# A rational activation rewritten in a scaled h: one square per unit, two output products, sums by accumulating transfers

## The chip, the cores and the metric

The kernel runs on one core of one Trainium2 chip. The metric is the device time of one execution in microseconds (us); lower is better. Three executions of the kernel before took 253.45, 253.46 and 253.82 us, median 253.46 us.

The core's engines work side by side, each through its own queue in order: TensorE (PE in the profile, its weight loads PEld), VectorE (DVE), ScalarE (ACT), GpSimd (POOL) and SyncE (SP). They wait for each other through semaphores. Transfers (DMA) are issued from the SyncE, ScalarE and GpSimd queues; those that add to what stands at their destination are issued from GpSimd here.

## The reference

Attention without softmax over a product of two sketches, and on its output a feed-forward layer whose activation is a rational function:

```python
def phi(x):                                   # x: (4, 4, 1088, 32), S1, S2: (8, 32)
    a = np.einsum('rd,bhsd->bhsr', S1, x)
    b = np.einsum('rd,bhsd->bhsr', S2, x)
    return np.einsum('bhsi,bhsj->bhsij', a, b).reshape(*x.shape[:-1], r * r)
q_p, k_p = (phi(q), phi(k))
kv = np.einsum('bhsf,bhsd->bhfd', k_p, v)
z = np.sum(k_p, axis=2)
num = np.einsum('bhsf,bhfd->bhsd', q_p, kv)
den = np.einsum('bhsf,bhf->bhs', q_p, z)[..., None] + 1e-06
attn_out = num / den

x = attn_out.transpose(0, 2, 1, 3).reshape(4352, 128)
h = x @ w_in                                  # w_in: (128, 2048)
P = a[0] + a[1] * h + a[2] * h * h + a[3] * h * h * h
Q = 1.0 + np.abs(b[0]) * np.abs(h) + np.abs(b[1]) * h * h
out = (P / (Q + 1e-6)) @ w_out                # w_out: (2048, 128)
```

## The kernel before

**Two halves that overlap.** The attention runs over four batches. For each, the keys (steps `K`) are turned, sketched, multiplied and summed into kv and z, and the queries (steps `Q`, in three or four pieces of tokens) are turned, sketched, multiplied with kv and z, divided and turned back into xT, which holds x with its 128 columns on the partitions (a ring of 1,536 tokens). The sketches of most query pieces go through DRAM: `dw` writes them, `dr` reads them back repeated over partitions. The feed-forward layer runs over 21 units. A unit is a stretch of tokens by a stretch of the 2,048 hidden columns; units 3 to 17 are 4,096 elements wide on each partition (512 tokens x 8 blocks of 128 columns, or 256 x 16), units 0 and 1 and 19 and 20 are 1,024 wide, units 2 and 18 are 2,048 wide.

**What a unit does.** The letters are those of the order below.
- `H`: TensorE makes h in parts of 1,024 elements into PSUM, in f32 (L518). `E`: ScalarE (or VectorE) copies a part to `hh` in bf16 (L272, L274).
- `U`: |h| on VectorE, by clearing the sign bit (L531). `W`: `w` = |b1| |h| + |b0| (L537, L539). `Y`: `w` times |h| (L554), so that w = |b1| h^2 + |b0| |h|. In units 6, 8, 10, 12 and 14 ScalarE instead takes a square of a scaled h (`D`, L544), and a transfer adds |h| to it (`M`, L550).
- `L`, `X`: r = 1 / (1 + w) on ScalarE, as Exp(-Ln(1 + 1e-6 + w)) (L576, L581). All Ln share one buffer.
- `P`: `g` = a3 h + a2 (L559, L562). `V`: `g` times h (L572). `A`, in units 7 to 15: a transfer adds a1, a constant tile in DRAM called `ones`, to it (L568). `S`: s = h r (L585). `G`: `g` times s (L589).
- `Or`, `Os`, `Og`: TensorE adds r, s and g times scaled copies of w_out to the output of the tokens in PSUM, 128 x 128 x 128 each (L620, L632). Units 7 to 15 have a1 in g and need only r and g, so two output products; most others need three. Units 16 and 17 need four, on r, s, s h and s h^2 (`B`, `C`, L594, L601), with two more scaled copies of w_out.
- `ST`, `OUT`: the output leaves PSUM and is stored.

**What sets the order.** All work is written out in one list of steps, `ORDER` (L40 to L78): a step's letter, the batch, piece or unit, the part, and the engine (`.a` ScalarE, `.d` VectorE) where there is a choice. Nothing else schedules. Each engine takes its own steps in this order, so a step that waits holds up all that follow on the same engine. The bf16 tiles stand in pools of their own: three buffers of `hh`, two of `w`, four of `g`, two of `r`, two of `s`, one of `u`, 14 of 8 KB per partition in all. `early` (L165) issues the first loads, `absolute`, `nearest` and `square_root` (L712 to L733) make the constants from a and b, `w_part` (L687) scales the copies of w_out.

Of the kernel before, what the change touches and what calls it, by code (L numbers as in the profile page):

```python
# [40 lines left out]
I0 I11 I2 I3 I7 Z10 Z3 K0.T0 K0.T1 SS0 K0.s0 K0.T2 F1.k K0.s1 K0.c1.a Q0.1.T Q0.1.sk Q0.1.c.a K0.c0.d I9 Q0.0.T  # L41
Q0.0.sk Q0.0.c.a K0.f0 K0.p0 K0.f1 Q0.2.T Q0.3.T Q0.0.f Q0.1.f K0.p1 I4 Q0.2.sk K1.T2 K0.k0.a Q0.0.p I8 KA0 K1.T1
K1.s1 Q0.0.pl.d Q0.0.r Q0.0.x Q0.2.c.a K1.c1.a Q0.0.b Q0.1.p K1.T0 Q0.1.pl.d I5 Q0.1.r Q0.0.kk.a I6 Q0.2.dw Q0.3.sk
F1.q Q0.3.c.d H0.0 Q0.1.x F1.v KA1 KA2 Q0.1.b AB0 K1.s0 w0.a Q0.2.dr w2.d w4.d E0.0.a H1.0 RT0 I10 U0.0.d K1.f1 W0.0.a
Y0.0 K1.c0.a K1.f0 H2.0 F2.k E1.0.a U1.0.d L0.0 Q0.1.kk.a Q1.2.T Q1.1.T H2.1 P0.0.d X0.0 W1.0.d E2.0.a Or0.0 E2.1.a
Q1.1.sk P1.0.a K1.p0 Q1.0.T Q1.0.sk Q1.0.c.a Y1.0 L1.0 Q0.3.dw V0.0 Q1.0.dw K1.p1 K1.k0.a S0.0 U2.0.d Q0.2.f Os0.0
Q0.2.p G0.0 X1.0 Q1.2.sk Or1.0 Q0.2.pl.d F2.q Q0.2.r Q0.2.x Q0.2.b Q0.3.dr V1.0 W2.0.a Q0.2.kk.d P2.0.d w3.a S1.0 V2.0
Og0.0 K2.T2 w5.a H3.0 w1.a E3.0.a H3.1 Q1.1.c.a Q1.2.c.a K2.T0 Q1.0.dr G1.0 Y2.0 E3.1.a L2.0 K2.s0 K2.c0.d K2.T1 H3.2
P3.0.d E3.2.a H3.3 E3.3.a Og1.0 X2.0 Q2.0.T Q2.0.sk H4.1 E4.1.a Q1.1.dw Q2.1.T P3.1.a Q2.2.T K2.f0 Q1.2.dw H4.0 E4.0.a
H4.2 E4.2.a U3.0.d W3.0.d Q2.0.c.a Y3.0 Os1.0 Q0.3.f Q1.0.f Q0.3.p K2.s1 V3.0 Q1.0.p Q1.0.pl.d Q0.3.pl.a Q0.3.r Q1.0.r  # L50
# [31 lines left out]
def kernel(  # L82
# [702 lines left out]
```

## Time and profile before

| what | us |
|---|---|
| median of the runs | 253.46 |
| runs, lowest and highest | 253.45, 253.82 |
| profiled execution: span from the first to the last instruction | 251.9 |
| busy: h_ps products (L518) | 127.5 |
| busy: ScalarE copies of h (L272) | 69.2 |
| busy: ScalarE Exp (L581) | 64.4 |
| busy: ScalarE Ln (L576, two groups) | 65.2 |
| busy: VectorE products s (L585) | 39.4 |
| GpSimd's accumulating transfers | 28, 512 KB each |

For the profiled execution the page gives its span, and no time around it. A row of a group gives line, engine, operation, output and inputs, sizes, a count, then busy time and the mean length of one, then the idle time just ahead of them and what ended it. A length is from start to end of one instruction; neighbours on one engine overlap a little, so that starts stand closer together than the lengths say. A row in order of time gives start and length in us. "DMA to landing" is the time from a transfer's issue to its last byte's arrival.

### The profile page before, as it was taken

How to read it: one execution, taken by the hardware profiler on the slowest of the kernel's cores; microseconds unless marked ns; L12 is line 12 of the kernel's file. 1: busy time of each engine (PE TensorE's matmuls, PEld its weight loads, DVE VectorE, ACT ScalarE, POOL GpSimd, SP SyncE). 2: the span in 40 equal slices, each digit the busy share in tenths (PEclk: the TensorE clock that was granted, in tenths of full speed). 3: DMA queues.
4: the chain of work that ended last, by engine and by line, in shares of the span. 5: the costliest groups of instructions: out<-in, count | busy, mean ns of one | idle time of the engine just before them, and what ended most of it. 6: DMA issues, size and time to landing. Idle time of an engine off the chain costs nothing.

```text
span 251.9 us, 6008 instructions
## 1 busy us (share of the span) xinstructions
PE 242.7 (96%) x2565; PEld 170.2 (68%) x2565; DVE 239.7 (95%) x231; ACT 231.5 (92%) x177; POOL 31.9 (13%) x61
## 2 busy tenths in 40 slices
PE   8999999999999999999999999999999889999994
PEld 2778844655575776756666578554675579999983
DVE  2889999999999999999999999999999999999993
ACT  2249999998999999999999999999999999999991
POOL 2140000000003000220242020350115300000000
PEclk9999999999999999999999999999999999999999
DMA  6986673378637468688759817899182995000300
GB/s 193 278 272 170 214 228 133 74 188 204 191 90 197 86 203 219 127 154 144 129 136 185 170 21 152 165 199 200 23 170 41 202 209 134 3 0 3 83 21 26
DMA packets 21834, 35.48 MB, mean 141 GB/s; under 512 B 2992, under 2 KB 13872, under 8 KB 21808
## 3 DMA queue, kind: packets, MB, share of 16 engines
q0 software_dynamic: 4032, 14.68, 31.3%
q1 hardware_dynamic: 16768, 19.80, 28.0%
q10 hardware_dynamic: 1008, 0.62, 1.1%
q8 instruction: 20, 0.33, 0.5%
q14 instruction: 6, 0.05, 0.1%
HBM read 26.12 MB, written 3.74 MB: 119 GB/s over the span
## 4 chain that ended last, share of the span: by engine, by line
ACT 36%; DVE 25%; PE 22%; issue 13%; DMA 2%; ACTq 0%; DVEq 0%
ACT hh L272 10%; PE h_ps L518 10%; ACT r L581 9%; ACT ln L576 8%; DVE g L572 4%; DVE w L554 4%; DVE g L589 3%; PE out_ps L632 3%; DVE u L531 3%; ACT w L544 3%; PE att_ps L433 2%; DVE s L585 2%; PE att_ps L337 2%; DMA s_raw<-in_S_dram 2%; DVE w L539 2%
## 5 line engine op out<-in xcount | busy, mean ns | idle before, releaser
L518 PE MATMUL h_ps<-xT,w_in_sb 128*128 128x512 f32 (+1 forms) x320 | 127.5, 539 | 2.4 <-ACT hh L272 1.8
L518 PEld LDWEIGHTS h_ps<-xT,w_in_sb 128*128 128x128 f32 x320 | 57.2, 190 | 45.6 <-issue 36.1
L272 ACT CAST hh<-h_ps 128x1024 bf16<-128x1024 f32 x66 | 69.2, 1122 | 1.0 <-PE h_ps L518 0.9
L581 ACT ACTIVATE r<-ln 128x4096 bf16<-128x4096 f32 (+2 forms) x21 | 64.4, 3068 | 0.1
L576 ACT ACTIVATE ln<-w 128x4096 f32<-128x4096 bf16 (+2 forms) x16 | 45.7, 2854 | 0.4 <-DVE w L554 0.4
L585 DVE TENSOR_TENSOR s<-hh,r 128x4096 bf16<-128x4096 bf16 (+2 forms) x21 | 39.4, 1874 | 0.1
L572 DVE TENSOR_TENSOR g<-g,hh 128x4096 bf16<-128x4096 bf16 (+2 forms) x19 | 34.7, 1830 | 0.0
L589 DVE TENSOR_TENSOR g<-g,s 128x4096 bf16<-128x4096 bf16 (+2 forms) x19 | 34.5, 1831 | 0.1
L632 PEld LDWEIGHTS <-r 128*128 128x128 bf16 x512 | 29.9, 98 | 6.8 <-issue 5.7
L632 PEld LDWEIGHTS <-g 128*128 128x128 bf16 x512 | 29.7, 98 | 4.5 <-issue 3.8
L554 DVE TENSOR_TENSOR w<-w,u 128x4096 bf16<-128x4096 bf16 (+2 forms) x16 | 27.9, 1746 | 0.0
L632 PE MATMUL out_ps<-w_out,r 128*128 128x128 bf16 x416 | 25.7, 219 | 0.0
L632 PE MATMUL out_ps<-w_out,g 128*128 128x128 bf16 x416 | 25.4, 219 | 0.0
L550 POOL DMA_DIRECT2D w<-u x10 | 9.9, 1195 | 110.5 <-DVE q_sb L366 58.8
L568 POOL DMA_DIRECT2D g<-ones x18 | 16.5, 1156 | 45.8 <-PE out_ps L632 19.3
L531 DVE TENSOR_SCALAR u<-hh 128x4096 uint16<-128x4096 uint16 (+2 forms) x21 | 21.2, 1010 | 1.0 <-ACT hh L272 1.0
L576 ACT ACTIVATE ln<-w,scale 128x4096 f32<-128x4096 bf16 x5 | 19.5, 3907 | 0.0
L544 ACT ACTIVATE w<-hh,root 128x4096 bf16<-128x4096 bf16 x5 | 19.2, 3848 | 0.0
L632 PEld LDWEIGHTS <-s 128*128 128x128 bf16 x288 | 16.7, 98 | 3.1 <-issue 2.9
L559 DVE TENSOR_SCALAR g<-hh,a_k 128x4096 bf16<-128x4096 bf16 (+2 forms) x16 | 18.6, 1166 | 0.0
L539 DVE TENSOR_SCALAR w<-u,b_abs 128x4096 bf16<-128x4096 bf16 (+2 forms) x13 | 15.3, 1174 | 0.1
L433 PE MATMUL att_ps<-kvz,a_all 128*64 128x66 f32 x288 | 10.9, 224 | 0.6 <-DVE a_all L417 0.2
(97 smaller groups left out, 219.0 us busy)
## 6 DMA issues: line engine op xcount, KB each, us to landing
g<-ones POOLq DMA_DIRECT2D x18, 512.0 KB, 8.1
w<-u POOLq DMA_DIRECT2D x10, 512.0 KB, 6.5
k_sb<-in_k_dram SPq DMA_DIRECT2D x4, 544.0 KB
a_all<-sk_d SPq DMA_DIRECT2D x6, 352.0 KB
b_all<-sk_d SPq DMA_DIRECT2D x12, 176.0 KB
q_sb<-in_q_dram SPq DMA_DIRECT2D x3, 544.0 KB
v_sb<-in_v_dram SPq DMA_DIRECT2D x10, 144.0 KB
out_dram<-out_sb SPq DMA_DIRECT2D x19, 64.0 KB
```

The costliest lines, as they stand in the source:

```text
L272: nc.scalar.copy(out=out, in_=in_)
L518: nc.tensor.matmul(t[:, (x - part * m) * tl:(x - part * m + 1) * tl], lhsT=w_in_sb[:, (f0 + x) * 128:(f0 + x + 1) * 128], rhs=xT[:, p:p + ...
L531: nc.vector.tensor_scalar(out=at(i, "u", *c).bitcast(U16), in0=at(i, "hh", *c).bitcast(U16), scalar1=0x7FFF, scalar2=None, op0=AX.bitwise_and)
L539: nc.vector.tensor_scalar(out=at(i, "w", *c), in0=at(i, "u", *c), scalar1=ab1, scalar2=ab0, op0=AX.mult, op1=AX.add)
L544: nc.scalar.activation(out=at(i, "w", *c), in_=at(i, "hh", *c), func=ACT.Square, scale=root)
L554: nc.vector.tensor_mul(out=at(i, "w", *c), in0=at(i, "w", *c), in1=at(i, "u", *c))
L572: nc.vector.tensor_mul(out=at(i, "g", *c), in0=at(i, "g", *c), in1=at(i, "hh", *c))
L576: nc.scalar.activation(out=ln_sb[:, :ce - c], in_=at(i, "w", c, ce), func=ACT.Ln, bias=1.0 + 1e-6, scale=scale0 if i in SQ else 1.0)
L581: nc.scalar.activation(out=at(i, "r", c, ce), in_=ln_sb[:, :ce - c], func=ACT.Exp, scale=-1.0)
L585: nc.vector.tensor_mul(out=at(i, "s", *c), in0=at(i, "hh", *c), in1=at(i, "r", *c))
L589: nc.vector.tensor_mul(out=at(i, "g", *c), in0=at(i, "g", *c), in1=at(i, "s", *c))
L632: nc.tensor.matmul(outs[t0][:, m * 128:(m + 1) * 128], lhsT=z[:, m * 128:(m + 1) * 128], rhs=w, start=first and j == 0 and m == 0, stop=le ...
```

## The change

**The algebra.** The denominator of each attention output is multiplied by b0/b1 (absolute values, kept off zero), so that x, and with it h, comes out multiplied by b1/b0. With this scaled h, |b0| |h| + |b1| h^2 of the reference is (b0^2/b1) (|h| + h^2), and the numerator is a0 + outer h (constant + h + cubic h^2). So one square serves both:
- `N`: w = h^2, on VectorE (16 units) or ScalarE (units 1, 4, 5, 7, 11).
- `U`: u = |h|, as before. `M` (15 units) or `Y` (6): u plus w, by transfer or on VectorE.
- `L`, `X`: as before, Ln with the scale b0^2/b1 in all units.
- `P`: g = cubic w + constant, on VectorE in all units. `A` (15 units) or `V` (6): g plus h, by transfer or on VectorE; `ones` is gone, the transfer's source is the unit's own `hh`.
- `S`: h times r, now written over `hh`. `G`: g times that.
- `Or`, `Og` alone in every unit: r with a0 w_out, g with outer w_out. `Os`, `Om`, `On`, `B`, `C`, `D`, `W` and the third to fifth copy of w_out are gone.

**Buffers.** The pools of `hh`, `u`, `w`, `g`, `r`, `s` become one pool of 14 tiles of the same size; `w`, `u`, `g` and `r` are taken from it by step as `hh` is.

**Start.** b_sb is loaded ahead of everything else on the SyncE queue (`I12`), and its absolute value (`C0`) is taken on ScalarE before the load of S2 is issued there. The other constants (`C1` to `C6`) are some 18 small operations on GpSimd and two on VectorE, spread over the first steps.

**Order.** The whole of `ORDER` is new: which copies of h VectorE makes (8 parts in place of 2), where the attention's steps stand, and where the units'.

```diff
-HH, WB, GB, RB, SB, LN, AB, RING = 3, 2, 4, 2, 2, 1, 3, 1536
+BUFS, LN, AB, RING = 14, 1, 3, 1536
-TWO = (7, 8, 9, 10, 11, 12, 13, 14, 15)
-SQ = (6, 8, 10, 12, 14)
-FOUR = (16, 17)
+SMALL, TINY = 1e-10, 1e-12
 ORDER = """
-I0 I11 I2 I3 I7 Z10 Z3 K0.T0 K0.T1 SS0 K0.s0 K0.T2 F1.k K0.s1 K0.c1.a Q0.1.T Q0.1.sk Q0.1.c.a K0.c0.d I9 Q0.0.T
...
+I12 C0 I11 I0 I2 I3 I7 I8 I9 C1 K0.T0 Q0.1.T K0.T2 SS0 K0.T1 C2 Q0.0.T C3 C4 Z10 K0.s0 K0.s1 Q0.1.sk Q0.0.sk
+K0.c0.a K0.c1.a K0.f0 K0.f1 Q0.2.T Q0.3.T Q0.0.c.a K0.p0 Q0.2.sk Q0.3.sk K0.p1 Q0.1.c.a Q0.2.c.a w2.a K0.k0.a C5
+Q0.0.f Q0.3.c.a Q0.0.p Z3 I4 F1.k F1.q Q0.0.pl.a Q0.0.r Q0.0.x Q1.0.T Q1.1.T Q0.0.b Q1.0.sk Q1.1.sk Q0.2.dw I6
+Q0.3.dw I5 Q0.2.dr Q1.0.c.d K1.T1 Q0.1.f K1.T0 K1.T2 Q1.1.c.d Q1.2.T Q0.2.f Q0.0.kk.a H0.0 H2.1 Q0.1.p Q0.2.p
...
+Or6 X7 E10.2.a Q2.1.kk.a E10.0.a S7 Q3.1.f Q3.0.pl.d L8 H11.0 H11.1 Og6 A8 M9 E11.0.a E11.1.a ST6.a X8 N10.d U10
+P10.d Q3.0.r G7 S8 Q3.0.x G8 H11.2 Or7 H11.3 Or8 Q3.1.p Og7 Og8 Q2.2.b A10 M10 E11.2.a E11.3.a L9 N11.a ST8.a
...
+N15.d U15 S13 Og11 H16.3 H16.2 G13 E16.3.a E16.2.a H16.1 H16.0 Og12 M14 A14 M15 L14 E16.1.a E16.0.a ST12.a X14
+U16 N16.d H17.0 H17.2 E17.2.a E17.0.a P15.d S14 P16.d V15 G14 M16 Or13 H17.3 H17.1 L15 E17.1.a E17.3.a A16 H18.0
+H18.1 Og13 Or14 Og14 X15 E18.1.a E18.0.a L16 X16 N17.d U17 S15 N18.d P17.d U18 G15 P18.d S16 G16 M17 OUT12 OUT10
+Or15 H19.0 Or16 H20.0 Og15 Og16 E19.0.a L17 M18 A17 E20.0.d U19 N19.d N20.d P19.d U20 P20.d V19 Y20 M19 X17 L18
+X18 ST16.a L19 ST14.a X19 S17 G17 A18 L20 X20 S18 A20 S19 G18 G19 S20 G20 Or17 Or18 Og17 Or19 Og18 Or20 Og19
+Og20 OUT16 OUT14 ST17.a ST20 OUT17 OUT20
 """
...
             if eng == "d":
-                nc.vector.tensor_scalar(out=self.den[:tl, :T * H], in0=self.nv[:, :, D], scalar1=1e-6, scalar2=None,
-                                        op0=AX.add)
+                nc.vector.tensor_scalar(out=self.den[:tl, :T * H], in0=self.nv[:, :, D], scalar1=1e-6, scalar2=back_by[:tl],
+                                        op0=AX.add, op1=AX.mult)
...
     def at(i, key, c, ce):
-        w = UW if key in WHOLE else 2048
-        k = c // w
-        if (key, k) not in live[i]:
-            pool, bufs = homes[key]
-            live[i][key, k] = pool.tile([128, w], BF, name=key, bufs=bufs)
-        assert ce <= (k + 1) * w
-        return live[i][key, k][:, c - k * w:ce - k * w]
+        if key not in live[i]:
+            live[i][key] = late.tile([128, UW], BF, name="x", bufs=BUFS)
+        return live[i][key][:, c:ce]
...
+    def square(i, eng):
+        c = whole(i)
+        if eng == "a":
+            nc.scalar.activation(out=at(i, "w", *c), in_=at(i, "hh", *c), func=ACT.Square)
+        else:
+            nc.vector.tensor_mul(out=at(i, "w", *c), in0=at(i, "hh", *c), in1=at(i, "hh", *c))
...
+    def by_transfer(i, to, of):
+        for x in range(0, width(i), 2048):
+            e = min(x + 2048, width(i))
+            nc.gpsimd.dma_start(out=at(i, to, x, e), in_=at(i, of, x, e), accum_op=AX.add)
+
+    def by_vector(i, to, of):
+        c = whole(i)
+        nc.vector.tensor_add(out=at(i, to, *c), in0=at(i, to, *c), in1=at(i, of, *c))
+
+    def factor(i, eng):
+        c = whole(i)
         if eng == "d":
-            nc.vector.tensor_scalar(out=at(i, "g", *c), in0=at(i, "hh", *c), scalar1=a3, scalar2=a2,
+            nc.vector.tensor_scalar(out=at(i, "g", *c), in0=at(i, "w", *c), scalar1=cubic, scalar2=constant,
                                     op0=AX.mult, op1=AX.add)
...
+    def logarithm(i):
+        c, ce = whole(i)
+        nc.scalar.activation(out=ln_sb[:, :ce], in_=at(i, "u", c, ce), func=ACT.Ln, bias=1.0 + 1e-6, scale=slope)
+
+    def scaled(i):
+        c = whole(i)
+        nc.vector.tensor_mul(out=at(i, "hh", *c), in0=at(i, "hh", *c), in1=at(i, "r", *c))
...
+    stages = {"H": hidden, "E": evac, "N": square, "U": absolute, "M": lambda i: by_transfer(i, "u", "w"),
+              "Y": lambda i: by_vector(i, "u", "w"), "P": factor, "A": lambda i: by_transfer(i, "g", "hh"),
+              "V": lambda i: by_vector(i, "g", "hh"), "L": logarithm, "X": inverse, "S": scaled, "G": rational,
+              "Or": lambda i: gather(i, 0), "Og": lambda i: gather(i, 1), "ST": turn_out, "OUT": store, "F": fetch,
+              "I": early, "w": w_part, "Z": turn, "C": coefficients, "SS": sketch_weights}
```

More of the change, by code (lines that the diff above doesn't have):

```diff
@@ L46 @@
[L46 to L50, printed above, removed]
@@ L636, in turn_out @@
+        left[t0] -= n
+        for m, x in ([(m, x) for m in range(2) for x in range(n)] if end else
+                     [(m, x) for x in range(n) for m in range(tl // 128)]):
+            c = x * tl + m * 128
+            nc.tensor.matmul(outs[t0][m], lhsT=at(i, ("r", "g")[y], c, c + 128), rhs=w_sb[y][:, f0 + x, :],
+                             start=first and x == 0 and (end or m == 0),
+                             stop=left[t0] == 0 and x == n - 1 and (end or m == tl // 128 - 1))
     def turn_out(i, eng="d"):
@@ L717, in nearest @@
         if n == 0:
[L718 to L721 removed]
+            nc.scalar.activation(out=b_sb, in_=b_sb, func=ACT.Abs)
         elif n == 1:
[L723 to L727 removed]
```

291 lines of the change are left out of this document (94 added, 197 removed).

## The prediction

> **What bounds the kernel now.** I read the page's busy shares first, then busy time by stretches, then the groups by line with shapes kept apart, then the order in time of TensorE, ScalarE and SyncE at the places that the change touches.
>
> ```profile
> span 251.9 us, 6008 instructions
> PE 242.7 (96%) x2565; PEld 170.2 (68%) x2565; DVE 239.7 (95%) x231; ACT 231.5 (92%) x177; POOL 31.9 (13%) x61
> q0 software_dynamic: 4032, 14.68, 31.3%
> q1 hardware_dynamic: 16768, 19.80, 28.0%
> 0.00:20.00 20.00, 17.94 (x232) 12.08 (x233) 12.90 (x32) 6.76 (x16) 5.54 (x33) 1.00 0.82 245
> 60.00:100.00 40.00, 40.00 (x408) 25.67 (x406) 39.96 (x39) 39.57 (x30) 1.98 (x2) 1.00 0.64 165
> 100.00:140.00 40.00, 39.93 (x403) 27.10 (x401) 40.00 (x28) 40.00 (x26) 9.69 (x10) 1.00 0.78 147
> 240.00:252.00 12.00, 7.73 (x131) 7.12 (x128) 7.82 (x12) 5.96 (x8) 0.00 (x0) 1.00 0.09 23
> ```
>
> In the stretches the columns are PE, PEld, DVE, ACT, POOL, clock, DMA share, GB/s. Between 20 and 240 us TensorE, VectorE and ScalarE are all filled, so no engine alone is the bound: whatever takes work from one of them is lost unless the other two shrink as well. The clock is full throughout and is no part of the argument. The runs' median, 253.46 us, stands 1.6 us above this span (253.46 - 251.9), and I add that at the end.
>
> **Engine sums of the change.** TensorE loses every product with s (288 + 32 loads of s), nothing else.
>
> ```profile
> L632 PEld LDWEIGHTS <-s 128*128 128x128 bf16 x288 | 16.7, 98 | 3.1 <-issue 2.9
> L620 PE MATMUL end_ps<-w_out,s 128*128 128x128 bf16 x32 | 2.1, 219 | 0.0
> 216.76 1.95 PE L632 MATMUL end_ps<-w_out,r 128*128 128x128 bf16 x32
> 218.55 1.95 PE L518 MATMUL h_ps<-xT,w_in_sb 128*128 128x256 f32 x8
> 220.33 1.95 PE L632 MATMUL out_ps<-w_out,g 128*128 128x128 bf16 x32
> ```
>
> The starts are 1.79 us apart both for 32 output products (56 ns each) and for one 1024-wide part of the hidden product. So 320 x 0.056 = 17.9 us go.
>
> VectorE, by rows:
>
> ```profile
> L585 DVE TENSOR_TENSOR s<-hh,r 128x4096 bf16<-128x4096 bf16 x15 | 34.2, 2279 | 0.1
> L559 DVE TENSOR_SCALAR g<-hh,a_k 128x4096 bf16<-128x4096 bf16 x12 | 15.9, 1334 | 0.0
> L274 DVE CAST hh<-h_ps 128x1024 bf16<-128x1024 f32 x2 | 2.4, 1217 | 0.0
> L539 DVE TENSOR_SCALAR w<-u,b_abs 128x4096 bf16<-128x4096 bf16 (+2 forms) x13 | 15.3, 1174 | 0.1
> L554 DVE TENSOR_TENSOR w<-w,u 128x4096 bf16<-128x4096 bf16 (+2 forms) x16 | 27.9, 1746 | 0.0
> L572 DVE TENSOR_TENSOR g<-g,hh 128x4096 bf16<-128x4096 bf16 (+2 forms) x19 | 34.7, 1830 | 0.0
> L589 DVE TENSOR_TENSOR g<-g,s 128x4096 bf16<-128x4096 bf16 (+2 forms) x19 | 34.5, 1831 | 0.1
> ```
>
> Gone are W (15.3), the third and fourth products of units 16 and 17 (four of 2.28 us, 9.1), the copies of weights (2.2) and Y and V as they were (27.9 + 34.7). New are squares of eleven full, two half and three quarter units (29.6), seven full and five quarter sums that stay on VectorE (19.4), five more P (5.1), two more G (4.8), six more evacuations (7.3) and small copies (2): 68.2 against 88.9, about -21. The square and the sum are not in the trace; both read and write tiles of the shape of L585, and I take its 2279 ns. Below, a read of one tile twice could cost as little as the 1334 ns of L559 (11 x 0.95 = -10 us); above, nothing in these rows is dearer.
>
> ScalarE loses six evacuations, the W and P that it did, one full square less a quarter, a weight copy and copies of xT, some 24 us by the lengths of single instructions, some 22 without their overlap. It gains the scale in every Ln:
>
> ```profile
> L544 ACT ACTIVATE w<-hh,root 128x4096 bf16<-128x4096 bf16 x5 | 19.2, 3848 | 0.0
> L562 ACT ACTIVATE g<-hh,a_k 128x1024 bf16<-128x1024 bf16 (+1 forms) x4 | 6.7, 1683 | 0.0
> L576 ACT ACTIVATE ln<-w 128x4096 f32<-128x4096 bf16 x10 | 37.5, 3748 | 0.0
> L576 ACT ACTIVATE ln<-w,scale 128x4096 f32<-128x4096 bf16 x5 | 19.5, 3907 | 0.0
> ```
>
> Ten full Ln x 0.16 = 1.6 us, so about -20. All three sums fall by 18 to 21 us. If the whole of it came through, the time would be 253.5 - 18 to 20 = 234 to 235.
>
> **What does not come through.** The new order has to be walked. TensorE's work other than the parts of h and the output products is 242.7 - 68 x 1.785 - 1408 x 0.0558 = 42.7 us (68 parts; 544 products with r, 544 with g, 320 with s), and all of it stands before unit 16 in the new order. Before the end of step H16.2 the order has 58 parts (103.5 us) and 672 output products (37.5), and the first 20 us hold 2.1 us of idling (20 - 17.94). Sum: 42.7 + 103.5 + 37.5 + 2.1 = 185.8. The same sum for the kernel before (58 parts, 864 products) gives 196.6 for the start of H16.2; the trace has 197.2, so I add 0.6.
>
> ```profile
> 197.17 3.70 PE L518 MATMUL h_ps<-xT,w_in_sb 128*128 128x512 f32 x8
> ```
>
> From there ScalarE has, in the new order, ten evacuations, four full Ln and Exp, one half-width pair, two quarter pairs and three copies out of PSUM.
>
> ```profile
> 218.07 3.62 ACT L581 ACTIVATE r<-ln 128x4096 bf16<-128x4096 f32 x1
> 221.59 1.91 ACT L272 CAST hh<-h_ps 128x1024 bf16<-128x1024 f32 x2
> 223.39 3.63 ACT L576 ACTIVATE ln<-w 128x4096 f32<-128x4096 bf16 x1
> 231.47 1.92 ACT L576 ACTIVATE ln<-w 128x2048 f32<-128x2048 bf16 x1
> 245.06 1.06 ACT L581 ACTIVATE r<-ln 128x1024 bf16<-128x1024 f32 x1
> 248.58 0.64 ACTq L661 DMA_DIRECT2D out_dram<-last  x1
> ```
>
> From start to start that is 0.9 an evacuation, 3.6 a full Ln, 3.52 a full Exp, 1.8 and 1.0 for the narrower ones, 0.5 a copy: 9.1 + 28.5 + 3.7 + 3.9 + 1.6 = 46.8. ScalarE reaches E16.2 earlier by its own sum than TensorE does (its rows before that step, with 13 us of idling at the start, come to some 176), so some 10 us of its saving turn into waits for h; and after H16.2 TensorE has 10 parts and 416 products, 41 us, less than ScalarE's 46.8, and its last products wait for ScalarE's results, so that its own saving ends there. The path is TensorE up to unit 16, then ScalarE. Exp of unit 17 also takes the buffer that product Og16 reads; G16, Og15 and Og16 end about 1.2 us after Ln of unit 17, so 1.2. After the last Exp the kernel before needs 251.9 - 246.1 = 5.8; S19, G18 and G19 stand just ahead of S20 here, so 6.1.
>
> **The start.** In the new order b_sb is SyncE's first load, and the absolute value of it on ScalarE waits for that load ahead of the load of S2 and two parts of v on the same queue.
>
> ```profile
> 0.72 0.41 SPq L130 DMA_DIRECT2D k_sb<-in_k_dram  x1
> 1.42 0.58 ACTq L147 DMA_DIRECT2D s_raw<-in_S_dram  x1
> 4.67 1.17 DVE L299 STREAM_TRANSPOSE k_p<-k_sb 128x512 f32<-128x512 f32 x2 [3.56 <-DMA k_sb<-in_k_dram]
> 6.78 0.21 DVE L225 STREAM_TRANSPOSE sT<-s_raw 128x32 f32<-128x32 f32 x1 [0.84 <-DMA s_raw<-in_S_dram]
> 16.27 1.99 PE L518 MATMUL h_ps<-xT,w_in_sb 128*128 128x256 f32 x8
> ```
>
> k moves back by one issue, 0.45 us. S2 takes 5.3 us from issue to use here; issued after b_sb has landed (2 to 4 us by the 3.9 us of the much larger k), it arrives 1 to 3 us later, and the first sketches with it. Then TensorE's first hidden product stands behind sketches of batch 1, whose q can be loaded only once batch 0's q has been transposed: an issue near 13.4, a landing 4 us later as for k, two transposes, two sketches, so H0 near 18.8 instead of 16.3. I take 2.5 us (0.5 to 4). TensorE being the first part of the path, it all counts.
>
> Sum: 185.8 + 0.6 + 2.5 + 46.8 + 1.2 + 6.1 = 243.0; with 1.6 it is **244.6 us**. The remaining edits (constants on GpSimd in the start, den on 12 numbers with two scalars, weights in two products) lie beside the waits for loads there; without that cover the constants cost their some 18 instructions of 0.2 us.
>
> **The transfers.** 28 accumulating transfers become 53, which are 51.5 of the old size.
>
> ```profile
> DMA to landing us min/median/max: 4.5/6.5/10.8
> DMA to landing us min/median/max: 5.2/8.1/12.0
> g<-ones POOLq DMA_DIRECT2D x6, 512.0 KB, 9.1
> L550 POOL DMA_DIRECT2D w<-u x10: 852/1042/2152, 77.6 to 182.5; - x10
> ```
>
> The first two lines are w<-u and g<-ones over the run, the third the burst of six between 190 and 212 us. One transfer fills all 16 engines for 31.3% x 251.9 / 28 = 2.8 us, so 51.5 take 145 us beside q1's 70.5 (28.0%): 216 of 243. That is 89%, so it fits, but without air. The median landing is covered: by the sums of rows, Ln follows the later of U and N by 6 to 16 us in the new order, and ScalarE's 10 us of waiting for h come on top. A burst landing of 9.1 eats some of it; if the cover were gone, each full M would cost its 6.5 to 9.1 us.
>
> The Trainium skill (SBUF — State Buffer, "SBUF: two separate sides") says that GpSimd cannot write the descriptors of its transfers while VectorE runs in a two-port mode, so that an issue waits for the VectorE instruction. This trace bears it out only in its longest issue, 2.15 us against a shortest of 0.85; by the rule at its worst the four issues of a turn of the loop below would cost 5 us of its spare 9.6. That adds nothing to the sum, and keeps the loop's chance from being smaller.
>
> **Rivals.** (a) The sums come through: ScalarE's order bends and the tail overlaps, 234 to 238. For it speaks that the kernel before keeps three engines filled; against it the 46.8 us after E16.2, which nothing shortens. 0.12. (b) The queue takes ScalarE's slack: at one transfer per 3.1 us (six in about 18.5 us from the first issue of the burst), the 45 from M5 on, at about 66 us, need 140, with 28 of q1's 70.5 (its packets after 66 us) 168, so the last lands at 234, and G20 and the tail after it end no sooner than the 243 of the sum; each further miss of Ln is paid. Two such misses at the 2.6 us between burst and median: 248 to 252. 0.20. (c) Slower, by one loop: P10 writes the buffer that Og6 reads (so it is in the built kernel, and much the same at P9, U11 and N13), A10 stands ahead of M10 on the GpSimd queue, Ln 10 waits for M10, Or10 for Exp 10. A turn is P 1.3, issues 1.8 each pair, two pairs landing in about 13, Ln and Exp 7.5, S and G 4.6, products 3.6: about 34 us, against four units of 10.9 us each (four parts and 64 products), 43.6. It decides once the two pairs land later than 23 us after the first issue; at a turn of 48 it is 1.1 us more for each of eleven units, 244.6 + 12 = 257. For it: a largest landing of 12.0 with half as many transfers. Against it: the burst's six still landed at 9.1. 0.12.
>
> **Numbers.** The forecast has 0.56, within 241 to 248. Less than 0.2% (0.5 us) can't be told from no change in this kernel. Faster: 0.56 + 0.12 + 0.17 of (b) = 0.85; same 0.03; slower 0.12. The range 239.5 to 253 leaves out most of (a) and all of (c).
>
> **What would show it.** Right: busy near 225 (PE), 219 (DVE), 211 (ACT); waits of ScalarE for h_ps of about 10 us in all, mostly before 190; the first hidden product near 18.8, H16.2 ending near 189; ACT filled from there to about 237; transfers landing in 7 to 10 us. Wrong: ScalarE waiting for a DMA in its Ln over 3 us in all (b), TensorE waiting in the middle for r or g (c), or the last hidden product and the last Exp within 10 us (a).

## The result and the profile after

| | kernel before | changed kernel | forecast |
|---|---|---|---|
| median us (lowest to highest) | 253.49 (253.45 to 253.82) | 262.43 (260.31 to 264.42) | 244.6 (239.5 to 253) |
| span of the profiled execution | 251.9 | 259.7 | 243.0 |
| mean granted clock of TensorE | 1.000 | 0.971 | full |

The ratio is 1.0324 with a 95% interval of 1.0285 to 1.0363: the change makes the kernel slower by 3.2%, where 3.5% faster was forecast. Medians hold all runs; a ratio leaves out runs more than 1.5% above the fastest of the same kernel (one of the changed kernel's four; two of four in e5_turn, e8_swap, e9_loads and e14_direct below, two of ten in e17_sum_adds, one of four in e3_both, e7_first_turn, e10_idle18, e11_start and e13_sum). Differences "by the ratios" are differences of two ratios times 253.5 us.

The page of the changed kernel, with busy sums, the clock in 40 slices, the queue of accumulating transfers, the chain and three groups:

```profile
span 259.7 us, 5402 instructions
...
PE 231.7 (89%) x2244; PEld 155.7 (60%) x2245; DVE 221.7 (85%) x223; ACT 212.4 (82%) x154; POOL 53.0 (20%) x94
...
PEclk9679799999999999999999999999999999999898
...
q0 software_dynamic: 7632, 27.00, 55.6%
...
PE 45%; ACT 26%; DMA 14%; issue 7%; DVE 5%; SPq 1%; ACTq 0%; DVEq 0%
...
L253 ACT CAST x<-h_ps 128x1024 bf16<-128x1024 f32 x60 | 60.6, 1035 | 14.3 <-PE h_ps L492 14.2
...
L531 ACT ACTIVATE ln<-x,slope 128x4096 f32<-128x4096 bf16 (+2 forms) x21 | 64.8, 3086 | 0.3 <-DMA x<-x 0.2
...
x<-x POOLq DMA_DIRECT2D x50, 512.0 KB, 7.2
```

The sums of work fell as forecast: VectorE by 18 us (239.7 to 221.7), ScalarE by 19 (231.5 to 212.4), TensorE by 11. But over the span no engine is filled any more (89, 85 and 82%); only TensorE still is, and only from 100 to 150 us. The stretches say where (columns as in the prediction), first the kernel before, then the changed kernel:

```profile
20.00:40.00 20.00, 19.65 (x201) 13.33 (x199) 19.65 (x34) 20.00 (x25) 0.00 (x0) 1.00 0.67 204
...
150.00:200.00 50.00, 49.41 (x420) 31.76 (x419) 49.97 (x39) 50.00 (x29) 11.73 (x14) 1.00 0.75 141
```

```profile
0.00:20.00 20.00, 14.35 (x162) 9.59 (x163) 7.21 (x18) 5.25 (x11) 6.08 (x41) 0.83 0.66 184
20.00:40.00 20.00, 16.93 (x150) 12.31 (x149) 14.01 (x32) 9.22 (x12) 1.05 (x1) 0.91 0.94 248
40.00:60.00 20.00, 19.25 (x163) 10.06 (x164) 18.92 (x27) 18.41 (x20) 1.75 (x2) 1.00 0.92 195
60.00:100.00 40.00, 37.89 (x382) 22.91 (x378) 34.46 (x37) 35.05 (x27) 6.99 (x8) 1.00 0.95 213
100.00:150.00 50.00, 50.00 (x544) 33.23 (x543) 47.37 (x40) 47.11 (x30) 12.25 (x14) 1.00 0.90 185
150.00:200.00 50.00, 46.08 (x365) 28.34 (x363) 46.39 (x35) 45.79 (x28) 11.25 (x14) 1.00 0.80 152
```

In the first 40 us TensorE is idle 8.7 us (5.65 + 3.07) and ScalarE works 14.5 us, where the kernel before had 26.8. Two waits, of 3.94 and 2.40 us (below), are 6.3 of the 8.7. Then there are 0.75 and 2.1 us of TensorE's idling to 100, none to 150, and 3.9 from 150 to 200, in a stretch where all three engines lose together.

TensorE's order in time of the start and at two places later (start, length, instruction, and in brackets the idle time ahead of it and who ended it):

```profile
9.57 2.19 PE L287 MATMUL att_ps<-S,k_p 128*64 128x64 f32 x36 [3.94 <-DVE S L219]
11.69 3.79 PE L364 MATMUL h_ps<-ln,SAB 64*128 64x256 f32 x16
...
22.27 3.72 PE L492 MATMUL h_ps<-xT,w_in_sb 128*128 128x256 f32 x16
...
29.02 0.75 PE L414 MATMUL att_ps<-kvz,a_all 128*64 128x66 f32 x16 [2.40 <-DVE a_all L398]
...
30.28 3.28 PE L492 MATMUL h_ps<-xT,w_in_sb 128*128 128x256 f32 x8
...
159.86 1.98 PE L492 MATMUL h_ps<-xT,w_in_sb 128*128 128x512 f32 x4 [1.89 <-ACT x L253]
...
199.48 3.65 PE L492 MATMUL h_ps<-xT,w_in_sb 128*128 128x512 f32 x8
```

The first sketches stand behind a wait of 3.94 us, the 16 products after them take 3.79 us at half clock (2.00 us at full clock in e3_both below), H0.0 starts at 22.27 and not at 18.8, and H16.2 (the second half of the last row) ends at 203.1 and not at 188.9.

### The profile page after: what moved, and what is told of

Same layout as the page of the kernel before. It is cut to its first block, busy times and chain, and to the rows that moved or that the text cites. A ratio compares the mean times of both kernels' runs of the same rounds, so it can differ in the third digit from the quotient of the medians.

```text
span 259.7 us, 5402 instructions
## 1 busy us (share of the span) xinstructions
PE 231.7 (89%) x2244; PEld 155.7 (60%) x2245; DVE 221.7 (85%) x223; ACT 212.4 (82%) x154; POOL 53.0 (20%) x94
## 3 DMA queue, kind: packets, MB, share of 16 engines
q0 software_dynamic: 7632, 27.00, 55.6%
## 4 chain that ended last, share of the span: by engine, by line
PE 45%; ACT 26%; DMA 14%; issue 7%; DVE 5%; SPq 1%; ACTq 0%; DVEq 0%
PE h_ps L492 23%; ACT x L535 10%; ACT ln L531 9%; PE out_ps L561 8%; ACT x L253 6%; DMA q_sb<-in_q_dram 5%; DMA v_sb<-in_v_dram 4%; PE end_ps L561 3%; PE att_ps L318 3%; PE att_ps L414 2%; DMA s_raw<-in_S_dram 2%; DMA b_all<-sk_d 2%; PE att_ps L287 2%; PE h_ps L364 1%; DVE x L539 1%
## 5 line engine op out<-in xcount | busy, mean ns | idle before, releaser
L515 POOL DMA_DIRECT2D x<-x x53 | 46.9, 1097 | 179.2 <-DVE x L509 34.3
L561 PEld LDWEIGHTS <-x 128*128 128x128 bf16 x1088 | 63.7, 99 | 15.9 <-issue 6.9
L253 ACT CAST x<-h_ps 128x1024 bf16<-128x1024 f32 x60 | 60.6, 1035 | 14.3 <-PE h_ps L492 14.2
L531 ACT ACTIVATE ln<-x,slope 128x4096 f32<-128x4096 bf16 (+2 forms) x21 | 64.8, 3086 | 0.3 <-DMA x<-x 0.2
L535 ACT ACTIVATE x<-ln 128x4096 bf16<-128x4096 f32 (+2 forms) x21 | 62.8, 2990 | 2.7 <-DVE x L505 2.6
L561 PE MATMUL out_ps<-w_out,x 128*128 128x128 bf16 x832 | 50.4, 219 | 0.0
L539 DVE TENSOR_TENSOR x<-x 128x4096 bf16<-128x4096 bf16 (+2 forms) x21 | 39.5, 1879 | 3.6 <-ACT x L535 3.6
L543 DVE TENSOR_TENSOR x<-x 128x4096 bf16<-128x4096 bf16 (+2 forms) x21 | 39.3, 1873 | 0.2
L505 DVE TENSOR_TENSOR x<-x 128x4096 bf16<-128x4096 bf16 (+2 forms) x16 | 29.5, 1852 | 1.6 <-ACT x L253 1.6
L524 DVE TENSOR_SCALAR x<-x,a_k 128x4096 bf16<-128x4096 bf16 (+2 forms) x21 | 23.7, 1132 | 2.0 <-PE out_ps L561 2.0
L509 DVE TENSOR_SCALAR x<-x 128x4096 uint16<-128x4096 uint16 (+2 forms) x21 | 21.3, 1013 | 0.8 <-ACT ln L531 0.8
L519 DVE TENSOR_TENSOR x<-x 128x4096 bf16<-128x4096 bf16 (+1 forms) x12 | 19.2, 1607 | 0.0
```

The source lines that it names most:

```text
L253: nc.scalar.copy(out=out, in_=in_)
L505: nc.vector.tensor_mul(out=at(i, "w", *c), in0=at(i, "hh", *c), in1=at(i, "hh", *c))
L509: nc.vector.tensor_scalar(out=at(i, "u", *c).bitcast(U16), in0=at(i, "hh", *c).bitcast(U16), scalar1=0x7FFF, scalar2=None, op0=AX.bitwise_and)
L515: nc.gpsimd.dma_start(out=at(i, to, x, e), in_=at(i, of, x, e), accum_op=AX.add)
L524: nc.vector.tensor_scalar(out=at(i, "g", *c), in0=at(i, "w", *c), scalar1=cubic, scalar2=constant, op0=AX.mult, op1=AX.add)
L531: nc.scalar.activation(out=ln_sb[:, :ce], in_=at(i, "u", c, ce), func=ACT.Ln, bias=1.0 + 1e-6, scale=slope)
```

## The experiments

The theory from these views: three losses that the sum did not hold, in the start (8 us), between 150 and 200 us (4), and in the last 55 us (2.5). The rival is the transfers: the 53 of them take 55.6% of the 16 DMA engines' time (row q0).

**The start and the transfers.** In `e1_idle` 18 idle products, not 10, reach up to the sketches; in `e2_s2` the second sketch matrix and k are loaded ahead of b_sb, as before the change; `e3_both` has the second edit and 13 idle products; `e4_none` leaves all 53 accumulating transfers out, and its sums with them.

```diff
-I12 C0 I11 I0 I2 I3 ... C4 Z10 K0.s0
+I11 I0 I12 C0 I2 I3 ... C4 Z13 K0.s0
```

> Eight idle products more ahead of the first sketches (18 in place of 10), nothing else. Theory, the start: TensorE stood still from 5.6 to 9.6 us, its granted clock then read 0.50 between 10 and 15 us, and the first sketches took 2.19 and 3.79 us where they took 1.27 and 1.93 before. With idle products until 9.2 us the clock stays at 1.00, H0 starts some 3 us sooner (19 in place of 22.3), and the end comes 2 to 3 us sooner: 259 to 260. Rival, the transfers: the DMA engines are 93 to 95% busy between 20 and 100 us and their landings set the end; a sooner start only waits longer for them, the time stays at 262.

> The loads of S2 and of k stand ahead of b_sb and its absolute value again; still 10 idle products. Theory, the start: the transposed S2 is there at 6.8 us in place of 9.1, TensorE stands still for under 2 us, its clock holds, and H0 starts near 17.5; of the 10 us that TensorE was late at H1.0 some 5 go: 257. Rival, the transfers: no change, 262.

> S2 and k ahead of b_sb, and 13 idle products as in the kernel before. Theory, the start: as without the three idle products, or up to 0.5 us less if the clock still dipped there: 256.5 to 257. Rival, the transfers: 262.

> All 53 accumulating transfers are left out, so that h squared is missing from 15 denominators and h from 15 numerators; the rest, the late start too, is as in the changed kernel. Theory, the start: H0 still starts at 22.3 and H1.0 at 33.8, and only what was lost later (some 3 us between 70 and 100 us and in the tail) can go: 256 to 260. Rival, the transfers: without them the time comes near the forecast, 245 to 250.

Measured: 259.34, 258.95, 259.4 and 260.11, with ratios of 1.0218 (1.0154 to 1.0282), 1.0212 (1.0145 to 1.0278), 1.0225 (1.0205 to 1.0246) and 1.0245 (1.0205 to 1.0284). TensorE in e3_both's start (columns as above):

```profile
8.54 1.29 PE L287 MATMUL att_ps<-S,k_p 128*64 128x64 f32 x36 [1.67 <-DVE S L219]
9.76 2.00 PE L364 MATMUL h_ps<-ln,SAB 64*128 64x256 f32 x16
...
18.86 3.72 PE L492 MATMUL h_ps<-xT,w_in_sb 128*128 128x256 f32 x16
```

In e3_both H0.0 starts 3.4 us earlier and the products run at full clock, and the time falls by 2.5 us by the ratios (2.7 in e1_idle, 2.8 in e2_s2; the intervals allow 1.0 to 4.0 in e3_both, and more in the other two). Either edit does about that; the old load order with 13 idle products does no more. e1_idle came as expected; e2_s2 and e3_both were expected at 257 and at 256.5 to 257, and in e2_s2 TensorE still waited 3.29 us ahead of the first sketches, not under 2. Leaving the transfers out saves 2.0 us in all (the two intervals allow 0 to 4). Its profiled execution has a worse start than the changed kernel's, 1.2 us more idling and a clock of 0.83 from 20 to 40 us, although only one accumulating transfer is due there, so the 2.0 may be a little low. But neither is the 18 us, and the rival falls as the main cause: 245 to 250 was its time without transfers, 260.1 came. e4_none's stretches show besides that the loss from 150 to 200 has nothing to do with the transfers:

```profile
60.00:100.00 40.00, 39.74 (x395) 23.96 (x396) 36.72 (x39) 37.28 (x28) 0.00 (x0) 1.00 0.44 113
...
150.00:200.00 50.00, 46.09 (x363) 28.34 (x361) 46.62 (x35) 45.79 (x28) 0.00 (x0) 1.00 0.03 6
```

TensorE has 46.09 of 50 there without any transfer, 46.08 with them. Its loss between 60 and 100, on the other hand, is gone (39.74 against 37.89).

**The two buffers of the hidden products.** The built program tells what happens at 156 to 172 us. H12.1 is evacuated by VectorE (done at 157.5), and yet H12.3 waits for E12.2, the evacuation of H12.2 on ScalarE, which stands behind a 3.63 us Exp. The pool has handed H12.3 the buffer of H12.2 and leaves the other one empty. In the changed kernel this happens at ten places (H4.0, H5.3, H8.0, H9.3, H12.3, H13.2, H13.1, H17.3, H18.0, H19.0), in the kernel before at four. `e5_turn` makes the pool take turns, in the changed kernel; `e12_before_turn` does it in the kernel before.

```diff
     def wide():
-        return hps.tile([128, 1024], FP, name="h_ps")
+        turns[0] += 1
+        return hps.tile([128, 1024], FP, name="h_ps", tag=f"h_ps{turns[0] % 2}", bufs=1)
```

> The changed kernel with one thing added: the two PSUM buffers of the hidden products are taken strictly in turn. In the changed kernel the pool hands the same buffer to two products one behind the other at ten places (H4.0, H5.3, H8.0, H9.3, H12.3, H13.2, H13.1, H17.3, H18.0, H19.0; in the kernel before at four), and at each of them product and evacuation run one after the other while the second buffer stands empty. Theory 'buffer': TensorE's waits for ScalarE's evacuations go (5.1 us of its idle time in 140 to 240, most of it at H12.3 to H13.1 and from H17.3 on), and ScalarE's for h_ps shrink from 14 us to under 10; time 262.4 - 3 to 4 = 258.5 to 259.5. Rival 'sums': ScalarE, VectorE and TensorE are each busy for 18 to 20 of every 20 us from 100 us on, so what one wait gives back is lost at the next: 261.5 to 262.5.

> The kernel before with nothing but the two buffers of the hidden products in turn (its pool hands the same one out twice running at H6.3, H11.2, H14.1 and H16.0). Theory 'buffer' alone would take up to 1 us off: 252.5 to 253.3. Rival 'ScalarE and VectorE have no gap there to fill' (busy 50.0 of 50 us from 100 to 150 and from 150 to 200): 253.4 to 253.6.

e5_turn: 261.18 (257.3 to 263.33), ratio 1.0193 (1.0132 to 1.0253), 3.3 us less than the changed kernel by the ratios, but only 1.3 by the medians. Its stretch, and then its TensorE at the same steps:

```profile
150.00:200.00 50.00, 48.86 (x335) 28.30 (x334) 49.97 (x35) 49.28 (x30) 12.62 (x15) 1.00 0.85 161
```

```profile
155.25 1.98 PE L495 MATMUL h_ps<-xT,w_in_sb 128*128 128x512 f32 x4 [0.27 <-DVE x L255]
...
163.67 3.60 PE L495 MATMUL h_ps<-xT,w_in_sb 128*128 128x512 f32 x8
```

H12.3 now waits 0.27 us for VectorE in place of 1.89 for ScalarE, and all three engines get 2.8 to 3.6 us of the 50 back (this profiled execution is e5_turn's fastest). The expected size held by the ratio, which rests on two of the four times; the pair e6_first and e7_first_turn below repeats it. One part of the expectation did not: ScalarE's waits for h_ps are 13.6 us, not under 10; they lie elsewhere. In e12_before_turn buffers in turn make the kernel before *slower*, 255.74 (ratio 1.0091, 1.0076 to 1.0106), which neither theory had. (There, and in the runs from e9_loads on, the first two tiles are numbered the other way round, so that the second and the third take the same buffer.) TensorE's waits for ScalarE's evacuations grow from 1.8 us to 4.7 there. I take it that an order made for the pool's choices loses when they change; no run shows it by itself. Taking turns is a cure for this order, not a rule.

**Another order of the start, and earlier loads.** `e6_first` puts H2.0 and H1.0 with their evacuations ahead of all that waits for a transfer; `e7_first_turn` adds the buffers in turn; `e8_swap` also fetches Q1.2 back ahead of batch 2's first sketches. (In these three, Ln 0 stands ahead of one weight table's first half and overwrites what it is made from, so those values differ; the work is the same.) `e9_loads` is e5_turn with the loads of the next batch issued early and the features of Q2.0 later, `e10_idle18` adds the start's load order and 18 idle products, `e11_start` a new order of the first 40 us.

```diff
-H5.0 Q2.0.dw Q2.0.dr F2.v F3.k Q2.1.dw Q1.2.dr F3.q
+H5.0 F3.q F2.v F3.k Q1.2.dr Q2.0.dw Q2.0.dr Q2.1.dw
```

> Second sketch matrix first and 13 idle products as in the third run, and now the hidden products of the first 256 tokens (H0.0, H2.1, H2.0, H1.0) with their evacuations ahead of everything that waits for the round trip of the sketches through DRAM: ahead of Q0.2's products on TensorE (which waited until 25.4 us there) and ahead of Q1.2's copy on ScalarE (which waited 6.3 us for a transfer, until 30.2 us, with two evacuations behind it). Theory 'order of the start': H3.0 starts 3 us earlier than there (32.4) and the end moves by 3 to 4: 255.5 to 256.5 against its 259.4. Rival 'sums': the gain is gone by 60 us; 258.5 to 259.5.

> The run before with the buffers of the hidden products in turn as well. Theory 'buffer and start are two causes': the gains add, 252 to 253.5. Rival 'sums': no more than the better of the two alone, 255.5 or more.

> The run before, with the third group of batch 1's queries fetched back (Q1.2.dr) ahead of batch 2's first group and ahead of the loads of batch 2, and the features of batch 2's first group (Q2.0.f) later. VectorE waited 5.0 us for that transfer at 69 us in the third run, and TensorE 3.0 us behind it at 76 us. Theory 'late fetch': 2 to 3 us less than the run before, 249.5 to 251. Rival 'hidden': under 0.5 us less.

> The changed kernel with the buffers in turn, and the loads of the next batch issued early: q of batch 3, v of batch 2 and k of batch 3 (F3.q, F2.v, F3.k) and then the fetch of Q1.2 stand on SP ahead of batch 2's sketches, whose fetch waits for a buffer; the features Q2.0.f are later. In the run before these loads were not moved, and the wait only went from one transfer (7.4 us for b_all) to another (7.8 us for q). Theory 'late loads': neither wait is there, TensorE is busy for 39.5 of the 40 us from 60 to 100 (39.1 in the run with the buffers in turn, 37.9 in the changed kernel), and the time is 255.5 to 258, with a smaller spread. Rival 'the wait moves on': another transfer is late by as much; 258.5 or more.

> The run before with the second sketch matrix's load first and 18 idle products, which reach to the first sketches. Theory 'start adds': the granted clock is 1.00 until 20 us, the 16 products of line 364's kind take 2.0 us and not 3.8, H0.0 starts near 19 and not 22, and the time is 3 less than the run before: 252.5 to 255. Rival 'lost later': within 1 of the run before.

> The run before with the first 40 us in another order: w_in's second and third load ahead of the sketches' writes on SP, H0.0 ahead of the sketches of batch 1, all four parts of the first 256 tokens and their evacuations ahead of what waits for a transfer, the write of Q1.0 and Q1.1 ahead of batch 1's v and batch 2's q. Theory 'order of the start': H3.0 starts near 29 to 30 (33.8 + in the changed kernel for H1.0, 36 for H3.0), and the time is 2 to 4 less than the run before: 249.5 to 252.5, less than the kernel before. Rival 'hidden by the queues': within 1 of the run before.

All six missed what was expected of them: 262.15, 259.4, 263.29, and then 270.89, 267.45 and 271.22. Two pairs among them still repeat a cure in another order: by the ratios the buffers in turn take off 3.5 us (e6_first, 1.0339, to e7_first_turn, 1.0202), and load order and idle products 2.0 us (e9_loads, 1.0609, to e10_idle18, 1.0532). SyncE's queue in e9_loads, ScalarE there, and SyncE in e5_turn, on which it is built, show why the last three are so slow:

```profile
39.19 1.27 SPq L395 DMA_DIRECT2D b_all<-sk_d  x2
...
57.11 0.33 SPq L123 DMA_DIRECT2D q_sb<-in_q_dram  x1
...
61.76 2.72 SPq L384 DMA_DIRECT2D sk_d<-sk_sb  x2
```

```profile
72.11 0.30 ACT L253 COPY sk_sb<-att_ps 128x176 f32<-128x176 f32 x1 [10.61 <-DMA sk_d<-sk_sb]
```

```profile
43.53 1.87 SPq L383 DMA_DIRECT2D sk_d<-sk_sb  x2
```

There is one buffer for q, and F3.q waits in it for batch 2's last sketch. Issued early, it holds SyncE's queue from 40.5 to 57.1 us; the fourth write of sketches, behind it, goes out at 61.76 where e5_turn has it at 43.53, and ScalarE waits 10.6 us for it to free its buffer. I had taken q, v and k for double-buffered. e8_swap fell to a mild form of it: Q1.2's features came in time, but F3.q, now later, made VectorE wait 7.8 us. e6_first lost the clock in its start (0.75 from 10 to 20 us), so it tests less than it was meant to.

**Causes together, the round trip, the crowding.** `e13_sum` is the changed kernel with both cures, load order with 18 idle products (not run by itself) and buffers in turn. `e14_direct` computes the third query group without the trip through DRAM; `e15_adds` is e14_direct with four of the 30 sums (five of the 53 transfers) on VectorE, and `e16_ahead` puts H3.0 and H3.3 ahead there. `e17_sum_adds` is e13_sum with the same four sums on VectorE and no other edit.

```diff
-C6 M2 K1.c0.a ... F3.q A2 A1 N4.a ... K2.p0 A3 Y4
+C6 Y2 K1.c0.a ... F3.q V2 V1 N4.a ... K2.p0 V3 Y4
```

> The changed kernel with the two causes shown so far taken out together: the second sketch matrix first and 18 idle products (3.0 to 3.5 us alone), and the buffers of the hidden products in turn (3.3 us alone). Theory 'two causes': they add, 255.5 to 257, and a remainder of 10 us against the predicted 244.6 stands, most of it before H3.0 (near 34 us). Rival 'sums': no better than either alone, 258.5 or more.

> The run before, with the third group of batch 0's queries (tokens 512 to 767) computed without the round trip through DRAM, by 16 more products as the first two groups are (FIRST = 3; its write and fetch fall away), and the steps up to H3.0 in the order that this allows: H0.0, H2.1, H2.0, H1.0 without a wait for a transfer between them. Theory 'round trip': the changed kernel has less work ahead of H3.0 than the kernel before, and both wait for the same fetch (the features of Q0.2 at 28.2 and 27.9 us); without it H3.0 starts at 28 to 30, TensorE is busy 3 to 5 us more by 40 us, and the time is 3 to 5 less than the run before: 251 to 253.5. Rival 'other loads': H3.0 comes earlier but the next steps wait for q and k of batches 1 and 2 instead, offset at H6 as in the run before; within 1.5 of it.

> The run before with four of the sums by transfer (M2, A1, A2, A3) as additions on VectorE, which has room before 100 us. Theory 'the accumulating transfers crowd out the loads of batch 2 between 55 and 80 us': TensorE's loss in 60 to 100 (0.3 to 3.7 us in the runs so far) goes to under 0.5, and the time falls by 1 to 2. Rival 'VectorE is full': its 5.5 us more come back at the end; 1 to 3 more than the run before.

> The run with four sums on VectorE and the third group computed directly, with H3.0 and H3.3 and their evacuations ahead of the third sketch of batch 1, the table factors and the second Ln. There H3.0 was ready at 27 us and started at 32.5, behind a sketch that waited 2.2 us for its transpose. Theory 'round trip and too little cover': H3.0 starts at 28 to 29, TensorE is busy for 9.3 or more of the 10 us from 30 to 40 (7.2 there), the offset at H4 is 5 to 6.5 (9.2 there) and the time 3 less: 255.5 to 257. Rival 'next loads': the gain is taken back by 60 us, because q and k of batch 2 land when they did; 258.5 to 260.

> The run with the start's load order, 18 idle products and the buffers in turn (258.0), with the same four sums (M2, A1, A2, A3) on VectorE. Theory 'crowding': in that run TensorE lost 0.9 us from 60 to 100, so there is little to win, up to 1 us, and VectorE's 5.5 us more cost 1 to 2 in the last 60 us: 257.5 to 259.5, with a narrower spread. Rival 'the transfers are what spreads the times': faster by 1 to 3, 255 to 257.

e13_sum: 257.97 (255.39 to 259.48), ratio 1.0145 (1.0090 to 1.0199), 4.5 us less than the changed kernel by the ratios. That lies between 3.3, the larger of the two alone, and 6.0, their sum, as it lies between the 255.5 to 257 and the 258.5 of the expectation; the intervals allow either, so it is not shown that the two add in full. e14_direct is slower, 266.84 (1.0407), and e15_adds 259.41 (1.0231), 4.5 us apart by the ratios for four sums out of 30. VectorE's wait for the fetched sketches and the stretch from 60 to 80, first in e14_direct, then in e15_adds:

```profile
79.43 0.89 DVE L402 TENSOR_TENSOR a_all<-a_all,b_all 128x704 f32<-128x704 f32 x1 [12.22 <-DMA b_all<-sk_d]
```

```profile
60.00:80.00 20.00, 15.00 (x147) 9.05 (x143) 6.92 (x10) 17.37 (x14) 3.49 (x4) 0.97 1.03 232
```

```profile
69.11 0.89 DVE L402 TENSOR_TENSOR a_all<-a_all,b_all 128x704 f32<-128x704 f32 x1 [2.02 <-DMA b_all<-sk_d]
```

```profile
60.00:80.00 20.00, 18.44 (x214) 11.68 (x211) 17.00 (x18) 18.29 (x15) 1.97 (x2) 1.00 0.73 174
```

With the DMA engines at 1.03 of their share the fetch comes 10 us later than at 0.73: SyncE issues it 5.2 us later (64.93 and 59.70), and from issue to use it takes 14.5 us in place of 9.4. The profiled executions are the slowest of each kernel (268.48 and 260.68), so the 10 us is the most seen, and the 4.5 us is what stands for the rest. So the transfers do crowd the fetches, by a little or by 10 us as the order and the execution have it. TensorE's loss between 60 and 100 us, though, is 2.3 us in e15_adds, not the under 0.5 that was expected. The Trainium skill (DMA: Bandwidth & Descriptors, "Issuing engines are not separate DMA queues") says that DMAs from all issuers run on the same 16 engines and interleave there; these rows agree. The round trip stays open: H3.0 never got more than a few us ahead, since in e14_direct and e15_adds it stood behind a sketch that waited for its transpose, and e16_ahead (260.46, ratio 1.0276) got 2.0 us more work out of TensorE up to 40 us and lost 3.6 between 40 and 60, at a clock of 0.91; that the steps put behind H3.0 did it is argued. e17_sum_adds: 255.96 (253.45 to 258.2), ratio 1.0075 (1.0046 to 1.0103), 1.8 us less than e13_sum (the two intervals allow -0.3 to 3.9): the time is the rival's, 255 to 257. Its mechanism, that the transfers are what spreads the times, is not shown: ten times spread over 4.8 us here, four over 4.1 in e13_sum.

**Room at the end.** The page's name for who ended ScalarE's wait before Exp 17 is VectorE in one run and TensorE in the next; the built program has five releases in that wait, and the last is the buffer that Og16 reads. `e18_room` is e17_sum_adds with the result of Exp 17 in w_in's place, which is free by then, and 8 idle products in TensorE's wait before Q0.2's products.

```diff
     def at(i, key, c, ce):
+        if (i, key) == (17, "r"):
+            return w_in_sb[:, c // 2:ce // 2].bitcast(BF)
...
-H0.0 H2.1 Q0.1.p Q0.2.p
+H0.0 H2.1 Q0.1.p Z8 Q0.2.p
```

> The fastest kernel so far that holds the change (four sums on VectorE, buffers in turn, load order, 18 idle products: 256.0, 253.5 to 256.8), with two waits taken away. The result of Exp 17 goes to w_in's place, which is free from the last hidden product on (233 us), and not to the buffer that Og16 gives back; ScalarE waited 2.9 us for that, TensorE 3.8 us behind it, and the granted clock was 0.50 in the 5 us after, where 32 products took 3.6 us and not 1.95. And 8 idle products stand in TensorE's wait of 3.2 us before Q0.2's products, after which the clock was 0.71 for 5 us. Theory 'waits and the clock they cost': no slice of the clock under 0.9 from 20 to 35 and from 235 to 250, and 3 to 4 us less: 251.5 to 253. Rival 'the end hangs on VectorE': VectorE's last additions follow the Exp of units 18 to 20 and it has 13 us of work from 235 on; 254.5 or more.

253.71 us (252.78 to 256.56), ratio to the kernel before 1.0011 (0.9989 to 1.0033), 1.6 us less than e17_sum_adds by the ratios: half of what was expected, for two edits that were not run apart. ScalarE and then TensorE at the end of the changed kernel; the same two of e18_room; what TensorE does next there; and the chain of e18_room by engine:

```profile
241.22 3.62 ACT L535 ACTIVATE x<-ln 128x4096 bf16<-128x4096 f32 x1 [2.62 <-DVE x L505]
```

```profile
244.89 3.40 PE L561 MATMUL end_ps<-w_out,x 128*128 128x128 bf16 x32 [3.76 <-ACT x L535]
```

```profile
231.30 3.62 ACT L541 ACTIVATE w_in_sb<-ln 128x4096 bf16<-128x4096 f32 x1
```

```profile
234.98 1.96 PE L567 MATMUL end_ps<-w_out,w_in_sb 128*128 128x128 bf16 x32 [0.84 <-ACT w_in_sb L541]
```

```profile
238.96 1.08 PE L567 MATMUL end_ps<-w_out,x 128*128 128x128 bf16 x16 [2.02 <-ACT x L541]
...
241.16 5.89 PE L567 MATMUL end_ps<-w_out,x 128*128 128x128 bf16 x80 [1.13 <-DVE x L549]
```

```profile
PE 38%; DVE 28%; ACT 16%; issue 10%; DMA 5%; SPq 1%; DVEq 0%; ACTq 0%
```

ScalarE's wait is gone, TensorE's is 0.84 us, and the 32 products run at full clock; the clock stays at 1.00 from 20 to 40 us as well. But the loss moves on: behind them TensorE waits 2.02 and 1.13 us, and the 80 products after that take 5.89 us, where 80 times 56 ns are 4.5, at a clock of 0.66 from 240 to 245 us. So the expectation of no slice under 0.9 failed. In the last row VectorE has 28% (5% in the changed kernel), most of it between 150 and 230 us; near the end its additions and products of 232.8 to 241.1 us stand in the chain ahead of those 80 products, so the rival is half right. The version with all cures is level with the kernel before; no version beats it.

## Why the prediction was wrong

- **The engine sums (right).** Forecast busy 225, 219 and 211; measured 231.7, 221.7 and 212.4. TensorE's excess is the lowered clock: products that took 1.29, 2.00, 1.99 and 1.95 us at full clock in other runs took 2.19, 3.79, 3.28 and 3.40 here, 5.4 of the 6.9 us over 242.7 - 17.9 = 224.8. (VectorE's rows that go add up to 89.2, not 88.9; it changes nothing.)
- **"I take 2.5 us (0.5 to 4)" for the start: the step that failed most.** The first 40 us hold 8.7 us of TensorE's idling, and 0.9 + 1.8 + 1.3 = 4.0 us by the slow clock: 12.7, where the sum had 2.1 + 2.5. That is 8 of the 14.2 us by which H16.2 is late. The direction of each piece was there (S2 late, H0 behind sketches), but I carried over from the kernel before that idling ends at 20 us, and that the clock is "no part of the argument". Shown: the load order and the idle clock, 2.5 to 2.8 us (e1 to e3). Argued only: the rest, the wait for the sketches' fetch with less other work in front of it. The features of Q0.2 start at 28.2 us here, 3.23 us after VectorE's last work, and at 27.9 in the kernel before, which had filled all engines until then.
- **"The new order has to be walked": walked without buffers.** The sum took TensorE as running without a stall from 20 us to H16.2. From 100 to 150 us that is exact (50.00 of 50). Between 150 and 200 it missed 3.9 us, because the pool hands one h_ps buffer out twice running (e5_turn: 2.8 us back on TensorE), and between 40 and 100 2.9 us, from which the transfers' crowding of loads takes its part (e4_none loses 0.3 of 40 us, the changed kernel 2.1).
- **The account:** idle to 200 us 5.65 + 3.07 + 0.75 + 2.11 + 0 + 3.92 = 15.5, less the 2.1 + 2.5 + 0.6 of the sum, and 4.0 by the clock, make 14.3; H16.2 ends 203.1 - 188.9 = 14.2 late.
- **The tail (46.8 + 1.2 + 6.1 = 54.1)** took 259.7 - 203.1 = 56.6, 2.5 more. The 1.2 us for the buffer of Og16 was the right mechanism with the wrong size, 2.6 here and 2.9 in e17_sum_adds, and behind it TensorE waited 3.8 us and ran 32 products at about half clock (in e18_room that wait is 0.8, and a smaller one with a slow clock comes later).
- 14.2 + 2.5 = 16.7 = 259.7 - 243.0. Of the other 1.1 us to 262.4, 0.9 is the profiled execution (261.5) lying below the median, and 0.2 the time around its span, 1.8 and not 1.6.
- **Rival (b), the queue takes ScalarE's slack: wrong** in its mechanism. Ln waited 0.2 us for transfers in all; landings had a median of 7.2 us, as forecast. The transfers cost 2.0 us (e4_none), mostly between 60 and 100 us and through other loads, where no rival had looked. **Rival (c)** did not come either: no wait for r or g in the middle. The sign was missed by all of the cases but (c), which had it through a loop that did not occur; all rested on the same 2.5 us.
- **What stays open:** the cures take 8 of the 18 us off. e18_room's span, 251.2, is still 8.2 above the forecast's 243.0: H16.2 ends there at 195.4, 6.5 late, and the tail takes 1.7 more. No run took that out.

## What to carry to other kernels

Walk a new order with its buffers and its loads, not only with its durations: ask of each wait in the start what stood in front of it before and no longer does, and of each rotating buffer which instruction releases it in the built program. A load in an in-order queue may be moved ahead only as far as its buffer is free; past that it stops everything behind it (16.6 us of SyncE's queue in e9_loads). And a change that removes work from all three engines can still lose by the waits of its new order; here several of them, taken out one after another, brought 262.4 us down to 253.7, which is still no gain.

## What was unexpected in the hardware

TensorE's granted clock fell to 0.50 for 5 us after a wait of 3.94 us (10 to 15 us), and to 0.71 after one of 2.40 us (30 to 35 us); after a wait of 1.89 us in a full stretch it stayed at 1.00. In other runs it stayed at 1.00 after 2.82 us (e2_s2, before Q0.2's products) and after 2.98 us (e3_both, at 76.6 us), and was 0.66 after 2.22 us (e13_sum, 25 to 30 us): between 2 and 3 us the length of a wait alone does not tell. Nor is the clock's column always the safest sign: in e5_turn's start it reads 1.00, while the 36 and 16 products take 2.19 and 3.00 us (1.29 and 2.00 in e3_both). The changed kernel by stretches of 5 us:

```profile
10.00:15.00 5.00, 5.00 (x50) 4.11 (x46) 3.01 (x4) 0.56 (x2) 2.82 (x14) 0.50 0.88 269
...
30.00:35.00 5.00, 5.00 (x21) 3.96 (x19) 3.43 (x11) 1.43 (x3) 0.00 (x0) 0.71 0.97 259
```

The Trainium skill (TensorE: Matmul & The Clock Gate, "Why this matters for your kernels") asks for no idle gap over about 3 us between products. The 3.94 us and the 3.76 us of the tail agree; the 2.40 us would have been harmless by it and was not, so here the measurement decides. Also unexpected: the times of the changed kernel spread over 4.1 us and those of the kernel before over 0.4, and the version with all cures (e18_room) still spreads over 3.8; why is open.
